# One load of v per four heads, longer runs of q, another order of keys and queries, and a planner with new figures

## The chip, the cores and the metric

The kernel runs on one core of one Trainium2 chip. The metric is device time in microseconds (us) of one execution. Engines are named as in the profile: PE is TensorE, DVE is VectorE, ACT is ScalarE, POOL is GpSimd, SP is the engine that issues most DMAs here.

## The reference

Attention over 8 batches, 12 heads, 448 positions and 64 dimensions, with q and k normalised, and then a gated two-layer network over all heads of a position, which the kernel calls MoE:

```python
q_n, k_n = rmsnorm(q, g_q), rmsnorm(k, g_k)
attn = softmax(q_n @ k_n.T / sqrt(64))          # per batch and head
x = (attn @ v) as (batch, 448, 768)
xk = mu_k * x + (1 - mu_k) * x_prev             # x_prev: one position earlier
xr = mu_r * x + (1 - mu_r) * x_prev
k = relu(xk @ w_k)                              # 768 -> 1024
out = sigmoid(xr @ w_r) * (k * k @ w_v)         # 1024 -> 768
```

The weights come as 64-bit floats and are converted on the chip.

## The kernel before

**Tiles.** A pair is two heads of one batch (48 pairs), a quad is two pairs (24 quads). The 448 positions are 7 slots of 64; position r*7 + t is row r of slot t, and a tile holds two heads in its two halves of 64 partitions. Most products are made in f16 with a high and a low part (three matmuls for one), but the first three quads (U32) run in f32. For the first six quads (PE_T) q and k are transposed by PE; after that they are split in two f16 parts and transposed by DMA.

**Stages.** These are generators, and they run side by side:

- `load` fetches a quad's k and q; `stats` squares and sums them (ACT, POOL, DVE) and makes the reciprocal root on DVE; `preps` scales them, splits them (`nat`) and transposes them into `stk`.
- `vload` fetches v of one pair into one of two tiles `vf`, with four DMAs on SP, in runs of one row (256 bytes). `vprep` squares v (ACT), brings the row sums to all partitions with a small matmul on PE, makes a power-of-two scale on DVE and splits v into `vh` and `vl`.
- `scores` makes two 128x448 score tiles per group, seven groups per quad; `expo` takes the maximum (DVE) and the exponential (ACT); `probs` and `split` normalise, split and transpose the result into `pT`, by a DMA transpose on SP or, for some groups, on PE.
- `attends` multiplies `pT` with v, one product per pair (`ot`), and ACT copies it into `x`. For the f32 pairs small matmuls (`rb`) bring the row sums and DVE multiplies by them. `mix` then forms xk and xr per pair (`df`, `xk`, `xr`).
- `wload` and `weights` fetch and convert 20 weight tiles; their DMAs are issued by ACT.
- `moe` runs the three matrix products: K (`mm<-xk,wk`), R (`mm<-wr,xr`) and V (`mm<-wv,kk`), and stores the output. K of a batch needs `xk` of its six pairs and all eight tiles of w_k; R and V of the first batch need all weights.

**What sets the order.** A planner (`Plan`) holds a clock per engine and prices every operation. Among the next operations of all generators it takes the one with the smallest start time less a priority, and appends it to its engine's program. Each engine then runs its program in that order, and waits on semaphores only. Priorities (`PRIO_`), margins (`MARGIN`) and boosts (`BOOST_`) are numbers at the head of the file, and so are leads (`LEAD_W`: the quad whose load must have begun before weights are fetched). The DMA figures, time to issue, to move and to land, stand in `emit`. Nearly all instructions are recorded by one line there (L272), so groups are told apart by their tiles. SP runs one queue: loads of q, k and v, transposes into `pT` and `stk`, and stores.

Two places of the memory matter for the change: v has `VF_BUFS` tiles `vf` and `VH_BUFS` tiles each of `vh` and `vl`; a `vf` tile is free again when its last reader is done (for f32 pairs that is the attention product itself).

Of the kernel before, what the change touches and what calls it, by code (L numbers as in the profile page):

```python
# [16 lines left out]
P = 128  # L17
HD = 64
# [6 lines left out]
NH = D_MODEL // 2  # L25
TINY = 2.0 ** -60
# [14 lines left out]
VF_BUFS = 2  # L41
# [4 lines left out]
PRIO_P = 200  # L46
PRIO_S = 150
PRIO_A = 50
PRIO_Q = 50
PRIO_V = 310  # L50
MARGIN = 600
MARGIN_A = 400
MARGIN_V = 1200
# [5 lines left out]
PRIO_O = 300  # L59
# [3 lines left out]
BOOST_R = 500  # L63
BOOST_A = 0
BOOST_W = 300
BOOST_Q = 600
SLACK_S = 3
SLACK_Q = 2
BOOST_V = 0
SLACK_V = 2  # L70
# [4 lines left out]
PRIO_L = 0  # L75
# [3 lines left out]
V_SIDE = 2  # L79
# [6 lines left out]
BOOST_F = 4000  # L86
# [4 lines left out]
LEAD_W = 1  # L91
# [3 lines left out]
W_GAP = 10e3  # L95
# [20 lines left out]
def heads(tile_, off):  # L116
    ap = tile_[:, :, :]
    return bass.AP(tensor=ap.tensor, offset=ap.offset + off, ap=[list(ap.ap[0]), [HD, 2], [2 * HD, NT], [1, HD]])
# [86 lines left out]
class Plan:  # L205
# [60 lines left out]
    def emit(self, ops):  # L266
# [18 lines left out]
        elif ops[0].fn.__name__.startswith("dma"):  # L285
# [3 lines left out]
            if "transpose" in op.fn.__name__:  # L289
                w, iss, tot = n / 128 * 1.21, 1600, 4000  # L290
            else:
                w, iss, tot = n / 55, 640, 3300
            w, tot = w * DMA_SLOW, tot * DMA_SLOW
            other = "ACT" if e == "SP" else "SP"
            if e == "ACT":
                end = s + (375 if n > 60000 else 610)
            else:
                end = max(s + iss, min(self.dma_free[e] - 1200, s + 4000))
# [122 lines left out]
def attn_moe_kernel(tc, q, k, v, g_q, g_k, mu_k, mu_r, w_k, w_v, w_r, out):  # L421
# [37 lines left out]
    NQ, NPAIR, NSS, NSL = len(quads), len(pairs), 4 * NT, (NT + 1) // 2  # L459
    VFREE = [const.tile([P, 2 * NSL, HD], F32, name="vf%d" % n) for n in range(VF_BUFS)]  # L460

# [17 lines left out]
    def late():  # L479
# [11 lines left out]
        "vh": Ring(ap_, [P, 2 * NSL, HD], F16, "vh", VH_BUFS, plan),  # L491
        "vl": Ring(ap_, [P, 2 * NSL, HD], F16, "vl", VH_BUFS, plan),
# [39 lines left out]
    def setup():  # L532
# [4 lines left out]
        for vf in VFREE:  # L537
            yield G_.memset(out=vf[HD:P, NSL - 1, :], value=0.0)
            yield G_.memset(out=vf[0:HD, NSL, :], value=0.0)
# [37 lines left out]
    def load():  # L577
        for u in range(NQ):
# [3 lines left out]
            for n, src in enumerate((k, q)):  # L582
                t = yield from R["qk"].get(u < 3)
                for x in range(2):
                    D = (A if u == 0 and (x or n == 0) else SP).dma_start
                    h0 = 4 * j + 2 * x
                    if u < PE_T or n == 0:
                        yield D(out=t[x * HD:(x + 1) * HD], in_=src[b, h0:h0 + 2].rearrange("h (r t) d -> r h (t d)", t=NT))
                    else:
                        tf = t.rearrange("p h c -> p (h c)")  # L590
                        for t0 in range(x, NT - 1, 2):
                            o = t0 // 2 * 4 * HD
                            yield D(out=tf[x * HD:(x + 1) * HD, o:o + 4 * HD].rearrange("p (h d) -> p h d", d=HD),
                                    in_=src[b, 4 * j:4 * j + 4].rearrange("h (r t) d -> r h t d", t=NT)[:, :, t0, :])
                        yield D(out=tf[x * HD:(x + 1) * HD, 12 * HD:].rearrange("p (h d) -> p h d", d=HD),
# [619 lines left out]
```

## Time and profile before

| | |
|---|---|
| median of 3 runs | 1036.73 us (1035.93 to 1038.05) |
| profiled execution, span | 1038.0 us; no time beside the span is given for it, so the span stands for its time |
| mean granted TensorE clock | 0.970 |
| busy: PE, DVE, ACT, POOL | 935.8, 788.0, 749.4, 661.0 us |
| DMA packets | 447,043, of which 418,784 are under 512 bytes |
| first MoE matmul (K) | at 166.64 us |
| start of the last attention product | at 934.35 us |

Busy time of an engine is not its limit: a matmul's end is modelled, and matmuls are pipelined. A row of waits reads: engine and tile, who released it, us in total, times, longest. A row of the timeline reads: start, duration, engine, line, operation, output and inputs, and in brackets the engine's idle time before it and who ended that. "SPq" and "ACTq" are the queues that issue DMAs.

### The profile page before, as it was taken

Reading aid. Unit: us, or ns where it says so; the run is one execution under the profiler, and the core shown is the slowest. Engines: PE = TensorE matmul, PEld = TensorE weight load, DVE = VectorE, ACT = ScalarE, POOL = GpSimd, SP = SyncE. Lnnn points to the kernel's source line nnn. Section 1 sums busy time; section 2 is a strip of 40 time slices with the busy share of each in tenths; the row PEclk is TensorE's granted clock in tenths of the full one; section 3 lists DMA queues with packets and bytes.
Section 4 is the critical chain, followed back from the end, with each engine's and each line's share of the span. In section 5 each row is a group of like instructions: output and inputs, shape, how many; then the busy total and the mean of one; then the engine's idle time right before and its main releaser. Section 6 shows DMA issues by size and latency. Waiting matters only on the chain. (4 is left out here: it accounts for less than half of the span.)

```text
span 1038.0 us, 19082 instructions
## 1 busy us (share of the span) xinstructions
PE 935.8 (90%) x6262; PEld 495.5 (48%) x6262; DVE 788.0 (76%) x1973; ACT 749.4 (72%) x1755; POOL 661.0 (64%) x696
## 2 busy tenths in 40 slices
PE   1778677879999999999999999899989999999997
PEld 1444433435554555454545544455545554555564
DVE  4898879998978897978895988779876879673000
ACT  2787657997968887888887886987887787873311
POOL 2564658936678567877677757855984757646501
PEclk9898887989999999999999999999999999999999
DMA  8543437988897999789798798799869977771011
GB/s 198 143 122 106 115 91 166 202 160 155 156 174 125 176 183 161 139 156 179 157 175 140 152 185 167 129 171 183 173 118 159 170 154 135 139 140 32 1 31 31
DMA packets 447043, 146.63 MB, mean 141 GB/s; under 512 B 418784, under 2 KB 443360, under 8 KB 446944
## 3 DMA queue, kind: packets, MB, share of 16 engines
q1 hardware_dynamic: 427408, 127.42, 65.7%
q10 hardware_dynamic: 19536, 18.00, 6.1%
q8 instruction: 49, 0.80, 0.3%
q14 instruction: 50, 0.41, 0.1%
HBM read 50.40 MB, written 11.01 MB: 59 GB/s over the span
## 5 line engine op out<-in xcount | busy, mean ns | idle before, releaser
L272 PE MATMUL mm<-wvh,kk 128*128 128x384 f16 x896 | 233.8, 326 | 0.6 <-POOL kk L272 0.4
L272 ACT ACTIVATE sc<-sc,sums 128x448 f32<-128x448 f32 x294 | 180.9, 617 | 59.2 <-DVE sums L272 54.8
L272 DVE TENSOR_REDUCE sums<-sc 128x1 f32<-128x448 f32 x336 | 194.8, 614 | 28.7 <-PE sc L272 27.9
L272 PE MATMUL mm<-xk,wkh 128*128 128x448 f16 x768 | 209.0, 354 | 3.8 <-ACT kf L272 2.6
L272 DVE SCALAR_TENSOR_TENSOR nat<-sc,sums,nat 128x448 f16<-128x448 f32 x246 | 161.2, 675 | 29.1 <-ACT nat L272 28.6
L272 ACT ACTIVATE nat<-sc,sums 128x448 f16<-128x448 f32 (+1 forms) x278 | 168.7, 648 | 14.2 <-DVE sums L272 4.9
L272 PE MATMUL mm<-wrh,xr 128*128 128x384 f16 x672 | 177.6, 329 | 0.0
L272 PEld LDWEIGHTS <-kk 128*128 128x128 f16 (+1 forms) x1362 | 129.5, 98 | 96.3 <-issue 14.4
L272 PE MATMUL sc<-stk 64*128 64x448 f16 (+3 forms) x1104 | 131.7, 385 | 22.1 <-DVE nat L272 12.7
L272 PE MATMUL mm<-wvl,kk 128*128 128x384 f16 x448 | 146.0, 326 | 0.0
L272 PE MATMUL mm<-xk,wkl 128*128 128x448 f16 x384 | 135.8, 354 | 0.0
L272 PEld LDWEIGHTS <-xr 128*128 128x128 f16 x1008 | 96.1, 98 | 73.9 <-issue 14.4
L272 PE MATMUL ot<-pT,vh 128*64 128x448 f16 x672 | 103.3, 364 | 11.1 <-DMA pT<-nat 7.4
L272 PE MATMUL mm<-wrl,xr 128*128 128x384 f16 x336 | 110.3, 328 | 0.0
L272 PEld LDWEIGHTS <-wkh 128*128 128x128 f16 x768 | 72.1, 98 | 79.1 <-issue 18.4
L272 DVE SCALAR_TENSOR_TENSOR o<-o,mm 128x384 f32<-128x384 f32 x56 | 30.7, 548 | 88.5 <-PE mm L272 58.5
L272 POOL TENSOR_TENSOR o<-o,bsc 128x384 f32<-128x384 f32 x48 | 42.9, 894 | 82.0 <-DVE o L272 49.3
L272 POOL TENSOR_TENSOR qk<-qk,ss 128x896 f32<-128x896 f32 x36 | 63.3, 1757 | 44.4 <-DVE ss L272 36.7
L272 ACT ACTIVATE o<-mm,bsc 128x128 f32<-128x128 f32 x144 | 44.6, 382 | 50.8 <-PE mm L272 38.6
L272 PEld LDWEIGHTS <-stk 64*128 64x128 f16 x1008 | 36.1, 98 | 80.2 <-issue 50.7
L272 DVE SCALAR_TENSOR_TENSOR df<-x,bsc,df 128x448 f32<-128x448 f32 x68 | 63.2, 941 | 5.4 <-POOL df L272 5.3
L272 POOL TENSOR_TENSOR nat<-nat 128x448 f32<-128x448 f32 x38 | 44.5, 1170 | 35.1 <-ACT nat L272 35.0
(169 smaller groups left out, 1784.5 us busy)
## 6 DMA issues: line engine op xcount, KB each, us to landing
out_dram<-o SPq DMA_DIRECT2D x56, 192.0 KB, 3.3
qk<-in_k_dram SPq DMA_DIRECT2D x46, 224.0 KB, 3.8
qk<-in_q_dram SPq DMA_DIRECT2D x108, 64.0 KB, 2.5
vf<-in_v_dram SPq DMA_DIRECT2D x96, 64.0 KB, 2.7
raw<-in_moe_w_v_dram ACTq DMA_DIRECT2D x12, 512.0 KB, 4.9
vf<-in_v_dram SPq DMA_DIRECT2D x96, 48.0 KB, 2.4
raw<-in_moe_w_r_dram ACTq DMA_DIRECT2D x12, 384.0 KB, 3.4
kk<-in_moe_w_k_dram ACTq DMA_DIRECT2D x8, 384.0 KB, 4.4
```

Source lines behind the costliest of these rows:

```text
L272: r = op.fn(op.kw["out"], op.kw["value"]) if op.fn.__name__ == "memset" else op.fn(**op.kw)
```

## The change

**v per quad.** One tile `vf` of a quad's size takes the place of two of a pair's size. Four DMAs load it, each for two heads in runs of 1024 or 768 bytes; one Square, one small matmul and one scale serve all four heads. `vh` and `vl` become one tile `vhl`, with two buffers still. The tile `vf` is free when both pairs are split (or, in f32, after both products and the Square).

**Order of keys and queries.** v's runs need the slots with even t side by side, then the odd ones: the order of keys (`KORD`) and of queries (`QORD`) follows. From quad 6 on q is loaded with one DMA of 768-byte runs and one of 256 per half, where there were three and one of 256. The f16 splits of k and q are made in two pieces each, and the copy of the attention product into `x` in two.

**The planner.** A transpose is priced at 1690 ns to issue and 4310 to land (1600 and 4000 before), a load at n/50 + 100 to move, 610 to issue and 2450 or 3300 to land (n/55, 640, 3300). Nearly all priorities, margins and boosts have other values, and weights are fetched one quad later (LEAD_W 2 for 1). Every engine's program comes out in another order.

```diff
-VF_BUFS = 2
+VF_BUFS = 1
-PRIO_P = 200
+PRIO_P = 447
-MARGIN_V = 1200
+MARGIN_V = 659
-LEAD_W = 1
+LEAD_W = 2
...
-                w, iss, tot = n / 128 * 1.21, 1600, 4000
+                w, iss, tot = n / 128 * 1.21, 1690, 4310
-                w, iss, tot = n / 55, 640, 3300
+                w, iss, tot = n / 50 + 100, 610, 2450 if n < 60000 else 3300
...
-                        for t0 in range(x, NT - 1, 2):
-                            o = t0 // 2 * 4 * HD
-                            yield D(out=tf[x * HD:(x + 1) * HD, o:o + 4 * HD].rearrange("p (h d) -> p h d", d=HD),
-                                    in_=src[b, 4 * j:4 * j + 4].rearrange("h (r t) d -> r h t d", t=NT)[:, :, t0, :])
+                        w = NLO * HD
+                        yield D(out=tf[xs, 0:4 * w].rearrange("p (h c) -> p h c", h=4),
+                                in_=src[b, 4 * j:4 * j + 4].rearrange("h (r t) d -> r h (t d)", t=NT)[:, :, x * w:(x + 1) * w])
...
-                yield A.copy(out=hi, in_=t4)
-                yield E_.tensor_tensor(out=lo, in0=t4, in1=hi, op=ALU.subtract)
+                for t4, hi, lo in views:
+                    yield A.copy(out=hi, in_=t4)
+                for t4, hi, lo in views:
+                    yield E_.tensor_tensor(out=lo, in0=t4, in1=hi, op=ALU.subtract)
...
-        for i in range(NPAIR):
-            b, hp = pairs[i]
+        for u in range(NQ):
+            b, j = quads[u]
             yield from until(lambda: VFREE)
             vf = VFREE.pop(0)
...
         if half:
             yield inverse(iv, sv)
-            yield A.activation(out=vh, in_=vf, func=AF.Copy, scale=sv)
-            yield V.scalar_tensor_tensor(out=vl, in0=vf, scalar=sv, in1=vh, op0=ALU.mult, op1=ALU.subtract)
+            for e in range(2):
+                if e:
+                    hl = yield from R["vhl"].get()
+                ve = vf[:, 2 * NSL * e:2 * NSL * (e + 1), :]
+                yield A.activation(out=hl[:, 0], in_=ve, func=AF.Copy, scale=sv)
+                yield V.scalar_tensor_tensor(out=hl[:, 1], in0=ve, scalar=sv, in1=hl[:, 0], op0=ALU.mult, op1=ALU.subtract)
             VFREE.append(vf)
```

Three places of the new order follow. First the head of ACT's program, before. Here `xk` and `nat` are lent as buffers: `xk_104` holds first the quad's k; `kk` and `raw` are lent for the first weight tiles.

```order
L272 DMA xk_104<-in_k_dram 64x2x448 x2
L272 ACT_TABLE_LOAD
L272 CAST ident_75<-ident 128x128
L272 DMA xk_104<-in_q_dram 64x2x448
L272 DMA kk_103<-in_moe_w_k_dram 128x3x256 x2
L272 DMA raw_135<-in_moe_w_k_dram 128x3x256
L272 DMA raw_138<-in_moe_w_k_dram 128x3x256
L272 ACTIVATE xk_104<-xk_104 128x896
L272 ACTIVATE nat_161<-xk_104 128x896
```

The same place now:

```order
L275 DMA xk_103<-in_k_dram 64x2x448
L275 ACT_TABLE_LOAD
L275 CAST ident_75<-ident 128x128
L275 DMA xk_103<-in_k_dram 64x2x448
L275 DMA xk_103<-in_q_dram 64x2x448
L275 ACTIVATE xk_103<-xk_103 128x896
L275 ACTIVATE nat_152<-xk_103 128x896
L275 DMA kk_102<-in_moe_w_k_dram 128x3x256 x2
L275 DMA raw_180<-in_moe_w_k_dram 128x3x256
```

The two Squares (of k, then of q) moved ahead of the four weight DMAs, and one half of k moved behind the cast.

Second, PE's program from the sixth attention product (`ot`) to the first K (`mm<-xk,wkh`), before. Each `sc` pair is one group of scores (6 or 12 matmuls with their weight loads, shown once), `rc` marks the `rb` matmuls, `wf` and `dg` are weight tiles.

```order
L272 MATMUL ot_1564<-pT,vf_95 64x448 x8
L272 MATMUL sc_1600<-stk_891 128x448
L272 MATMUL sc_1599<-stk_891 128x448
L272 MATMUL sc_1616<-stk_891 64x448
L272 MATMUL sc_1615<-stk_891 64x448
L272 MATMUL sc_1660<-ident,rc_107 64x128 x6
L272 MATMUL sc_1687<-stk_891 128x448
L272 MATMUL sc_1686<-stk_891 128x448
L272 MATMUL mm_1705<-wf_1552 128x128
L272 MATMUL mm_1705<-dg,ones 128x128
L272 MATMUL mm_1746<-xk_104,wkh 128x448
```

And now:

```order
L275 MATMUL ot_1512<-pT,vf_94 64x448 x8
L275 MATMUL mm_1507<-wf_1468 128x128
L275 MATMUL mm_1507<-dg,ones 128x128
L275 MATMUL sc_1527<-ident,nat_1495 128x128 x4
L275 MATMUL sc_1554<-stk_925 128x448
L275 MATMUL sc_1553<-stk_925 128x448
L275 MATMUL sc_1572<-ident,rc_106 64x2x64 x6
L275 MATMUL mm_1612<-wf_1547 128x128
L275 MATMUL sc_1620<-stk_925 64x448
L275 MATMUL sc_1619<-stk_925 64x448
L275 MATMUL mm_1612<-dg,ones 128x128
L275 MATMUL mm_1671<-xk_103,wkh 128x448
```

One group of scores stands ahead of `rb` where two stood, and two groups in all where three stood; a weight tile's matmuls and a transpose of four blocks came in ahead.

Third, SP's queue around one quad's q in the middle of the program, before:

```order
L272 DMA_TRANSPOSE stk_5207<-nat_5220 128x14x128
L272 DMA qk_5254<-in_q_dram 64x4x64 x3
L272 DMA qk_5254<-in_q_dram 64x2x64
L272 DMA_TRANSPOSE stk_5207<-nat_5296 128x14x128
L272 DMA qk_5390<-in_k_dram 64x2x448 x2
L272 DMA_TRANSPOSE pT<-nat_5209 128x14x128
```

Now:

```order
L275 DMA_TRANSPOSE stk_5156<-natx_5165 128x14x128
L275 DMA qk_5245<-in_q_dram 64x4x192
L275 DMA qk_5245<-in_q_dram 64x2x64
L275 DMA_TRANSPOSE stk_5156<-nat_5251 128x14x128
L275 DMA qk_5291<-in_k_dram 64x2x448 x2
L275 DMA_TRANSPOSE pT<-nat_5213 128x14x128
```

The rows of three q loads become one row of a single load with runs of three slots; the second half's loads repeat the first half's and are not shown.

More of the change, by code (lines that the diff above doesn't have):

```diff
@@ L25 @@
 NH = D_MODEL // 2
+NSL = (NT + 1) // 2
+NLO = NT // 2
+KORD = [t // 2 + NSL * (t % 2) for t in range(NT)]
+QORD = [t // 2 + NLO * (t % 2) for t in range(NT - 1)] + [NT - 1]
 TINY = 2.0 ** -60
@@ L671, in turn @@
                     o = column(z[:, a * P:], HD, 1)
-                ops.append(T.transpose(form=("tr", TR_COST), out=o, in_=w[:, a0 + a, :], identity=ident))
+                ops.append(T.transpose(form=("tr", TR_COST), out=o, in_=w[:, (QORD if n else KORD)[a0 + a], :], identity=ident))
             ops[0].form = ("tr", TR_COST * m)
@@ L711, in vfree @@
+            VF[u] = vf
+    def vfree(u, vf):
+        FR[u] = FR.get(u, 0) + 1
+        if FR[u] == 3:
             VFREE.append(vf)
     def vpreps():
-        i = 0
-        while i < NPAIR:
-            st["vi"] = i
-            n = V_SIDE if i < 2 * U32 else 1
-            yield from vprep([i + e for e in range(n)])
-            i += n
-    def vprep(js):
-        b, hp = pairs[js[0]]
-        n, half = len(js), js[0] >= 2 * U32
-        if hp == 0:
-            BS[b] = small.tile([P, 2 * NP], F32, name="bstat", bufs=3)
+        for u in range(NQ):
+            st["vi"] = u
+            yield from vprep(u)
@@ L726, in vprep @@
+    def vprep(u):
+        b, j = quads[u]
+        half = u >= U32
+        n = 1 if half else 2
+        NS = NP // 2 * n
+        if j == 0:
+            BS[b] = small.tile([P, 2 * NS], F32, name="bstat", bufs=3)
         s_ = BS[b]
         vs = small.tile([P, 4], F32, name="vs", bufs=4)
-        vh = vl = pt = None
-        for e, i in enumerate(js):
-            yield from until(lambda: i in VF and st["tq"] >= GATE_V)
-            vf = VF.pop(i)
-            if half:
-                vh = yield from R["vh"].get()
-                vl = yield from R["vl"].get()
-                sq = vh.bitcast(BF16)
-            else:
-                VV[i] = vf, None, None
-                pt = pt or (yield from banks["ot"].get())
-                sq = pt.rearrange("p (a c) -> p a c", c=HD)
-            yield A.activation(out=sq, in_=vf, func=AF.Square, accum_out=vs[:, e:e + 1])
-            if not half:
-                vfree(i, vf)
-                if e < n - 1:
-                    banks["ot"].put(pt)
-                    pt = None
@@ L746, in vprep @@
-        pt = pt or (yield from banks["ot"].get())
+        yield from until(lambda: u in VF and st["tq"] >= GATE_V)
+        vf = VF.pop(u)
+        hl = pt = None
+        if half:
+            hl = yield from R["vhl"].get()
+            yield A.activation(out=hl.rearrange("p a c d -> p (a c) d").bitcast(BF16), in_=vf, func=AF.Square, accum_out=vs[:, 0:1])
+            pt = yield from banks["ot"].get()
+        else:
+            for e in range(2):
+                VV[2 * u + e] = vf[:, 2 * NSL * e:2 * NSL * (e + 1), :], None, vf
+            pt = yield from banks["ot"].get()
+            for e in range(2):
+                yield A.activation(out=pt.rearrange("p (a c) -> p a c", c=HD), in_=vf[:, 2 * NSL * e:2 * NSL * (e + 1), :], func=AF.Square, accum_out=vs[:, e:e + 1])
+            vfree(u, vf)
@@ L904, in attends @@
             x = yield from R["x"].get()
[L905 removed]
+            vh, vl, own = VV.pop(i)
+            iv = None if vl is None else own[0]
             pT = PT.pop(i)
```

105 lines of the change are left out of this document (53 added, 52 removed).

## The prediction

> **What bounds the kernel now.** I read the page first, then the busy time by stage, then TensorE's waits in the early and in the long middle stage, then single stretches of the timeline.
>
> ```profile
> span 1038.0 us, 19082 instructions
> PE 935.8 (90%) x6262; PEld 495.5 (48%) x6262; DVE 788.0 (76%) x1973; ACT 749.4 (72%) x1755; POOL 661.0 (64%) x696
> ```
>
> TensorE (PE) is busy for 90% of the span, so 102 us is all that any order of the work can win without removing matmuls. The table of stages says where these 102 us lie:
>
> ```profile
> core 0: us, PE busy (x) PEld busy (x) DVE busy (x) ACT busy (x) POOL busy (x), PEclk, DMA share, GB/s
> 0.00:21.30 21.30, 0.00 (x0) 0.03 (x1) 9.68 (x39) 5.61 (x10) 5.62 (x16) 1.00 0.80 197
> 21.30:166.60 145.30, 107.73 (x674) 61.22 (x675) 124.61 (x359) 99.98 (x231) 83.99 (x94) 0.86 0.47 124
> 166.60:210.00 43.40, 36.89 (x249) 18.35 (x249) 40.20 (x85) 38.58 (x81) 38.18 (x40) 0.96 0.83 183
> 210.00:234.00 24.00, 17.36 (x122) 8.91 (x122) 23.01 (x70) 21.44 (x49) 7.85 (x10) 0.87 0.79 155
> 234.00:480.00 246.00, 239.94 (x1646) 124.65 (x1642) 208.16 (x503) 198.30 (x472) 174.12 (x174) 0.99 0.87 158
> 480.00:720.00 240.00, 228.58 (x1579) 118.33 (x1578) 197.88 (x487) 193.67 (x456) 166.67 (x169) 0.99 0.89 164
> 720.00:936.70 216.70, 209.61 (x1440) 108.96 (x1435) 170.69 (x417) 169.03 (x405) 147.57 (x155) 0.99 0.79 148
> ```
>
> Span less PE busy gives the idle time of each: 21.3 us before the first transpose, 37.6 us up to the first MoE matmul at 166.6, 13.1 us in the next two stretches together, and 6.1 + 11.4 + 7.1 = 24.6 us in the 702.7 us from 234 to 936.7. The rest, 5.7 us, lies at the very end. Up to 166.6 it is VectorE (DVE) that sets the pace: it is busy 124.61 of 145.3 us (86%) while PE has 74%. From 234 on PE is 96.5% busy and sets the pace itself. Its waits, first from 21 to 167 us, then from 234 to 937:
>
> ```profile
> PE sc L272 <- DVE nat L272: 29.9, 6, 21.3
> PE ot L272 <- DVE dg L272: 4.5, 1, 4.5
> PE sc L272 <- POOL nat L272: 4.2, 3, 1.8
> ```
> ```profile
> PE ot L272 <- DMA pT<-nat: 6.6, 8, 1.4
> PE sc L272 <- DVE nat L272: 5.3, 9, 1.2
> PE sc L272 <- DMA stk<-nat: 4.0, 4, 2.6
> ```
>
> The 29.9 hold the 21.3 us of the start. In the middle stage 10.6 of the 24.6 us are waits for DMA transposes.
>
> The other end of the program is fixed: from the last attention product on, PE runs matmuls alone.
>
> ```profile
> 936.74 88.78 PE mm L272 x522
> ```
>
> Both orders keep nearly the same work behind the last attention product: 564 matmuls then and 570 now, of which this row of the chain holds 522. So the total is PE's work plus PE's idle time, and each edit is priced by what it does to these two.
>
> **Part by part. The start.** The first transpose waits for q's sums of squares:
>
> ```profile
> 0.73 1.40 ACTq L272 DMA_DIRECT2D xk<-in_k_dram  x2
> 9.04 2.01 ACTq L272 DMA_DIRECT2D raw<-in_moe_w_k_dram  x2
> 11.10 0.95 ACT L272 ACTIVATE xk<-xk 128x896 f32<-128x896 f32 x1 [7.34 <-DMA kk<-in_moe_w_k_dram]
> xk<-in_k_dram ACTq DMA_DIRECT2D x2, 224.0 KB, 6.2
> 13.29 0.62 DVE L272 TENSOR_REDUCE sst<-xk 128x14 f32<-128x448 f32 x1 [2.59 <-POOL xk L272]
> 16.42 0.61 DVE L272 TENSOR_REDUCE sst<-nat 128x14 f32<-128x448 f32 x1
> 21.30 1.73 PE L272 MATMUL sc<-ident,nat 128*128 128x128 f32 x7 [21.30 <-DVE nat L272]
> ```
>
> The k tile was asked for at 0.73 and its second half 0.7 later; with 6.2 us to landing it is there by 7.6. Yet the first Square starts at 11.10, right behind the weight DMAs that ACT issues until 11.05. In the new order those four issues stand behind both Squares. One of the two k issues now stands behind the identity's cast; even if that costs it 1 us, k lands by 8.6 and its Square starts 2.5 us sooner. On DVE the small instructions on the gains no longer stand split around k's reduction, so q's reduction moves from 16.42 by about as much. I take **2.5 us** off the start; the ends are 0 (q's own half, issued last, lands as late as before) and 4.
>
> **Up to the first MoE matmul.** Counted in the two orders, the last mixing instruction of batch 0 on DVE (the sixth that writes `df`) is its instruction 388 before and 366 now: scores, a normalisation and a half-precision v of later quads moved behind it. By the stage's row an instruction of DVE takes 124.61/359 = 0.347 us, so 22 fewer are 7.6 us of DVE, 8.9 us of a stage in which DVE is 86% busy. Two more rows show how PE ends this stage:
>
> ```profile
> 159.47 1.96 PE L272 MATMUL sc<-ident,rc 128*64 128x128 f32 x16 [5.05 <-DVE nat L272]
> 166.64 0.90 PE L272 MATMUL mm<-xk,wkh 128*128 128x448 f16 x2 [0.38 <-DVE WSC L272]
> ```
>
> The `rb` matmuls of the sixth pair, which release its mixing, waited 5.05 us for a PSUM bank that DVE's splits held, because 18 score matmuls (two groups, four banks) stood in front. In the new order one group of 6 stands in front. On the other side, nine more weight matmuls and two more half weight tiles come ahead of the first MoE matmul, and what is postponed must be done later, where DVE is busy 40.20 of 43.40 us. There the MoE's R and V matmuls become available earlier in the program (after 96 attention matmuls in place of 144), so PE has something to fill with. I take **6 us**, between nothing and 10.
>
> **DMA and SP's queue, 234 to 937 us.** A quad's q took eight issues and takes four; its v took eight and takes four.
>
> ```profile
> q1 hardware_dynamic: 382610, 109.37, 84.7%
> qk<-in_q_dram SPq DMA_DIRECT2D x102, 64.0 KB, 2.5
> vf<-in_v_dram SPq DMA_DIRECT2D x72, 64.0 KB, 2.7
> pT<-nat SPq DMA_TRANSPOSE x108, 4.6
> ```
> ```profile
> L272 SPq DMA_DIRECT2D vf<-in_v_dram x192: 595/614/1560, 2.4 to 900.5; - x192
> L272 SPq DMA_TRANSPOSE pT<-nat x123: 1322/1866/3709, 153.8 to 928.8; - x123
> ```
>
> The transposes stand in the same queue as these loads. Eight issues less of 0.614 us per quad, over about 17 quads of this stage, take some 84 of 703 us from SP. The 16 DMA engines are busy 84.7% of the time with 382,610 packets, 24.9 ns of one engine each. Packets of v fall from 1792 to 512 per quad, of q from 1792 to 768: 39,000 fewer in 17 quads. If a packet costs the same whatever its size, that is 61 us of all 16 engines (9% of the stage); if only bytes count, nothing. Of PE's 10.6 us of waits for transposes I take **4 us** off, between 0 and 10.6; nearer the low end, because a transpose takes 1.87 us to issue and 4.6 us to land whatever stood before it.
>
> The Trainium skill, page "DMA: Bandwidth & Descriptors", section "Why small descriptors are slow (HBM only)", charges every packet about 3 cycles on top of one per 32 bytes, 11 for 256 bytes. By that a run of 768 bytes takes 27 cycles in place of 33, and these loads would keep 82% of their DMA time: an estimate from that page of 17 us of all engines in place of 61, and by it I would take 1 us here in place of 4, which makes the sum 12.5 and the time 1024. No row of this trace separates the two.
>
> **v's statistics.** One chain per quad replaces two, 21 times. PE loses 21 small matmuls:
>
> ```profile
> 181.87 0.22 PE L272 MATMUL ot<-ident,vs 128*128 128x128 bf16 x1
> 182.02 0.74 PE L272 MATMUL sc<-stk 64*128 64x448 f16 x6
> L272 DVE TENSOR_REDUCE vs<-ot 128x1 f32<-128x128 f32 x42 | 11.8, 280 | 6.2 <-PE ot L272 6.2
> ```
>
> The next matmul starts 0.15 us after it, and it can take its whole 0.22: 3.2 to 4.6 us of PE's own time. I take **3 us**. DVE loses 21 reductions of 0.280 and three small instructions with each, some 12 us spread over 700; DVE is 82% busy there, so I count nothing (at most 3 us less).
>
> **What is added.** Splitting the f16 copies of k and q (two pieces each, 18 quads) gives ACT and GpSimd (POOL) 36 instructions more each; the copy out of the attention product gives ACT 24 more; the one Square per quad takes 21 away.
>
> ```profile
> L272 ACT CAST nat<-qk 128x896 f16<-128x896 f32 x28 | 27.0, 965 | 3.8 <-POOL qk L272 2.1 <-POOL x L272 1.6
> L272 ACT CAST xk<-df 128x448 f16<-128x448 f32 x34 | 19.5, 578 | 5.8 <-DVE df L272 5.6
> L272 POOL TENSOR_TENSOR nat<-qk,nat 128x896 f16<-128x896 f32 x28 | 53.6, 1914 | 18.4 <-ACT nat L272 16.4 <-DVE nat L272 1.6
> L272 POOL TENSOR_TENSOR xk<-df,xk 128x448 f16<-128x448 f32 x34 | 37.9, 1116 | 17.3 <-ACT xk L272 13.7 <-DVE natx L272 3.5
> ```
>
> Two halves cost 2 x 578 - 965 = 191 ns more on ACT and 2 x 1116 - 1914 = 318 ns more on POOL: 39 x 0.191 = 7 us of ACT and 36 x 0.318 = 11 us of POOL in some 800 us. ACT is busy 80% and POOL 70% of the middle stage, and the pieces stand a quad ahead of the scores that need them: nothing, and up to 4 us if that lead is gone.
>
> **The sum.** 2.5 + 6 + 4 + 3 = 15.5 us off 1038.0, that is 1022.5 for the profiled execution, whose span stands 1.3 us over the runs' median of 1036.73. So **1021 us** for the median. Less than 0.2% (2 us) is what a measurement of this kernel cannot tell from no change.
>
> **The rivals.** *One v buffer on a shared queue.* Two v tiles of a pair become one of a quad. Its load may start only when the second pair's last read is done, and it waits at the head of SP's queue with transposes behind it. Four issues and a landing are 4 x 0.614 + 2.7 = 5.2 us. The 42 half-precision attention products between 166.6 and 936.7 come 18.3 us apart on average, which covers this, and in the order the two products of a quad stand close with a long gap to the next quad. But if the planner releases loads too early on SP, 5.2 us shows at each late quad: from three quads of 21 on the sum is eaten, with five it is 26 us, so 1021 + 26 = 1047. The Trainium skill, page "Trainium Kernel Development and Optimization", section "Best Practices", speaks for this rival: double-buffer, so that DMA and compute overlap; no row of this trace shows a load without its second buffer. I give it 0.13.
>
> *The gain is taken back.* The start (2.5) and the matmuls (3) hold, the rest is eaten by the postponed DVE work: 1031. For it speaks DVE's 93% right after 166.6. 0.17.
>
> *No net gain,* new waits in the new order cancelling it: 1037. 0.08.
>
> *More than forecast:* all terms at their upper ends, 4 + 10 + 10.6 + 4.6 = 29, or most of it: 1007 to 1012. 0.10.
>
> **How the numbers follow.** The forecast, 1021 with 1013 to 1029 of its own, has 0.52. Below 1010 and above 1040 I leave about 0.06 and 0.11; so 1010 to 1040. Faster is the forecast, the half gain and the large gain, 0.52 + 0.17 + 0.10 = 0.79; same 0.08; slower 0.13.
>
> **What would show it.** Right: the first transpose near 19 us and the first MoE matmul at 155 to 160; PE idle between 234 and the last attention product under 21 us, its waits for `pT` and `stk` transposes under 7; q1's share in that stage below 80%. Wrong: the first MoE matmul at 165 or later (the second term), waits of PE or ACT for `vf` DMAs or for `vh`/`vhl` that grow (the first rival), or PE idle over 25 us in the middle stage.

## The result and the profile after

The changed kernel takes **1002.68 us** (median of 4 runs, 998.37 to 1003.91) where the kernel before took 1037.39 beside it (4 runs, 1035.93 to 1040.87): a ratio of 0.9649, 95% interval 0.9622 to 0.9677. The forecast was 1021 with a range from 1010 to 1040, so the sign was right and the size, 15.5 us, less than half of the 35. The profiled execution took 998.37 us, 2 more than its span. It is the shortest of the four: the two profiled spans lie 41.6 us apart where the medians lie 34.7. The page begins:

```profile
span 996.4 us, 18699 instructions
PE 926.0 (93%) x6241; PEld 487.4 (49%) x6241; DVE 777.6 (78%) x1890; ACT 749.7 (75%) x1772; POOL 675.9 (68%) x732
```

The busy time by stage, cut at the first transpose, the first MoE matmul and the last matmul of the last attention product, and between them near the cuts of before, 200 for 210 among them (stretch, its length, then busy time per engine, granted clock, DMA share, GB/s):

```profile
0.00:18.91 18.91, 0.00 (x0) 0.03 (x1) 10.82 (x39) 5.78 (x9) 5.11 (x14) 1.00 0.77 198
18.91:151.00 132.09, 104.68 (x670) 59.74 (x671) 118.39 (x330) 94.08 (x216) 84.01 (x95) 0.90 0.51 138
151.00:200.00 49.00, 40.88 (x263) 20.59 (x262) 45.38 (x108) 42.49 (x88) 36.62 (x38) 0.96 0.73 163
200.00:234.00 34.00, 33.38 (x253) 18.33 (x251) 30.36 (x83) 30.90 (x78) 19.19 (x21) 1.00 0.81 150
234.00:480.00 246.00, 245.12 (x1699) 125.72 (x1698) 213.16 (x505) 208.99 (x504) 183.71 (x196) 1.00 0.92 172
480.00:720.00 240.00, 235.46 (x1611) 119.81 (x1610) 204.81 (x476) 203.81 (x487) 189.14 (x199) 1.00 0.91 169
720.00:893.80 173.80, 169.62 (x1187) 87.45 (x1181) 140.48 (x333) 140.82 (x341) 119.86 (x130) 1.00 0.80 151
893.80:996.40 102.60, 96.91 (x574) 55.69 (x570) 14.21 (x21) 22.82 (x55) 38.23 (x42) 0.99 0.10 24
```

The span fell by 41.6 us: 2.4 in the start, 13.2 up to the first MoE matmul (145.3 to 132.1), 27.0 up to the last attention product (769.8 to 742.8, with its last matmul at 936.4 and at 893.8), and 1.0 came back at the end. From 234 us on PE is idle for 9.6 us where it was for 24.6. Over the whole span its idle time went from 102.2 to 70.3 us, and its busy time from 935.8 to 926.1.

TensorE's waits, first from 18.91 to 151 us, then from 151 to 893 us (us in total, times, longest):

```profile
PE sc L275 <- DVE nat L275: 19.2, 2, 18.9
PE mm L275 <- DVE wf L275: 7.3, 3, 3.3
PE mm L275 <- DVE dg L275: 3.6, 4, 2.0
```
```profile
PE mm L275 <- ACT kf L275: 6.4, 2, 3.9
PE sc L275 <- DVE nat L275: 4.5, 8, 1.2
PE sc L275 <- POOL nat L275: 1.5, 3, 1.0
PE ot L275 <- ACT vhl L275: 1.2, 2, 0.7
PE ot L275 <- DMA pT<-nat: 1.2, 2, 0.6
```

The 19.2 hold the 18.9 us of the start. The waits for DMA transposes, 10.6 us from 234 us on before, are down to 1.2. The queue of the loads, in the stretch from 234 us to the last product:

```profile
q1 hardware_dynamic: 336215, 108.25, 87.8%
```

Packets are fewer (382,610 before), but the share of the DMA engines rose from 84.7% to 87.8%: 27.6 ns for a packet in place of 24.9. Times the length of the stretch, the queue's packets took 579 us of all 16 engines where they took 595; the stretch itself shrank by 43.

### The profile page after: what moved, and what is told of

It is laid out like the page before. It is cut to its first block, busy times and chain, and to the rows that moved or that the text cites. A ratio compares the mean times of both kernels' runs of the same rounds, so it can differ in the third digit from the quotient of the medians.

```text
span 996.4 us, 18699 instructions
## 1 busy us (share of the span) xinstructions
PE 926.0 (93%) x6241; PEld 487.4 (49%) x6241; DVE 777.6 (78%) x1890; ACT 749.7 (75%) x1772; POOL 675.9 (68%) x732
## 3 DMA queue, kind: packets, MB, share of 16 engines
q1 hardware_dynamic: 375568, 127.41, 67.4%
## 5 line engine op out<-in xcount | busy, mean ns | idle before, releaser
L275 ACT ACTIVATE sc<-sc,sums 128x448 f32<-128x448 f32 x294 | 182.1, 623 | 47.0 <-DVE sums L275 43.1
L275 ACT ACTIVATE nat<-sc,sums 128x448 f16<-128x448 f32 (+1 forms) x276 | 163.0, 647 | 22.3 <-DVE sums L275 16.1
L275 DVE SCALAR_TENSOR_TENSOR nat<-sc,sums,nat 128x448 f16<-128x448 f32 x242 | 154.6, 676 | 22.8 <-ACT nat L275 22.0
L275 PE MATMUL ot<-pT,vhl 128*64 128x448 f16 x1008 | 103.7, 354 | 2.9 <-DMA pT<-nat 1.2
L275 DVE SCALAR_TENSOR_TENSOR o<-o,mm 128x384 f32<-128x384 f32 x56 | 30.7, 548 | 89.1 <-PE mm L275 55.2
L275 POOL TENSOR_TENSOR qk<-qk,ss 128x896 f32<-128x896 f32 x36 | 62.8, 1745 | 32.4 <-DVE ss L275 26.5
L275 PEld LDWEIGHTS <-vhl 128*64 128x64 f16 x1008 | 54.7, 110 | 48.5 <-issue 8.9
L275 DVE SCALAR_TENSOR_TENSOR df<-x,bsc,df 128x448 f32<-128x448 f32 x68 | 71.2, 1057 | 8.3 <-POOL df L275 8.2
L275 POOL TENSOR_TENSOR nat<-qk,nat 128x768 f16<-128x768 f32 (+3 forms) x58 | 62.7, 1094 | 11.5 <-ACT nat L275 11.2
```

What stands on the lines that cost most here:

```text
L275: r = op.fn(op.kw["out"], op.kw["value"]) if op.fn.__name__ == "memset" else op.fn(**op.kw)
```

## The experiments

Two accounts stood against each other at the start. *Loads:* the new layout gives the gain through SP's queue or the packets, and the prediction priced it too low. *Order:* the planner's new numbers give it, and the layout little. A third held that v's statistics are worth more than 3 us. Measured, each beside the kernel before on the same chip; PE's idle time is a stretch's length less PE busy, in the four stretches (start, to the first MoE matmul, to the last attention product, behind it), and the last column counts PE's matmuls from the last one of the last product on. The last four columns are of the one profiled execution, which need not be the median one (that of e7 is its longest):

| run | median us (range, runs) | ratio, 95% interval | first MoE at | PE busy | PE idle | behind |
|---|---|---|---|---|---|---|
| before | 1037.39 (1035.93–1040.87, 4) | | 166.6 | 935.8 | 21.3+37.6+37.7+5.7 = 102.2 | 568 |
| after | 1002.68 (998.37–1003.91, 4) | 0.9649, 0.9622–0.9677 | 151.0 | 926.1 | 18.9+27.4+18.3+5.7 = 70.3 | 574 |
| e1_layout_only | 1033.71 (1030.33–1037.6, 10) | 0.9969, 0.9953–0.9985 | 171.9 | 936.9 | 20.9+38.6+32.0+5.7 = 97.2 | 570 |
| e2_planner_only | 1070.56 (1069.17–1076.33, 4) | 1.0338, 1.0304–1.0372 | 163.7 | 949.3 | 13.2+44.8+55.2+6.0 = 119.1 | 580 |
| e5_old_dma_figures | 1048.02 (1044.22–1049.58, 4) | 1.0106, 1.0072–1.0140 | 170.1 | 940.9 | 18.8+39.5+40.8+5.8 = 104.9 | 796 |
| e6_old_priorities | 1035.65 (1033.03–1039.73, 10) | 0.9996, 0.9978–1.0015 | 170.8 | 935.7 | 20.4+39.0+31.5+5.9 = 96.9 | 574 |
| e3_old_runs_same_order | 1066.22 (1061.18–1074.51, 4) | 1.0293, 1.0237–1.0349 | 153.4 | 947.6 | 18.7+27.8+67.7+5.7 = 119.8 | 574 |
| e7_q_old_runs | 1036.69 (1033.42–1044.4, 10) | 1.0014, 0.9988–1.0040 | 156.9 | 941.8 | 18.9+28.7+47.5+5.7 = 100.8 | 574 |
| f1_q_three_long | 1040.97 (1037.94–1048.44, 10) | 1.0021, 0.9999–1.0044 | 153.8 | 935.8 | 18.8+27.9+48.1+5.7 = 100.4 | 574 |
| e8_v_two_issues | 1019.83 (1017.94–1022.47, 4) | 0.9841, 0.9809–0.9874 | 151.1 | 934.0 | 18.3+28.7+33.9+5.7 = 86.7 | 576 |
| e14_v_half_on_act | 1002.32 (999.29–1008.55, 4) | 0.9666, 0.9627–0.9704 | 151.7 | 930.8 | 18.1+26.7+20.0+5.7 = 70.5 | 574 |
| f6_q_tail_on_act | 1000.93 (999.98–1002.4, 4) | 0.9650, 0.9621–0.9678 | 152.1 | 928.2 | 19.1+28.5+18.6+5.7 = 71.8 | 574 |
| e4_v_chain_twice | 1006.58 (1004.54–1010.0, 4) | 0.9721, 0.9694–0.9748 | 151.8 | 930.1 | 19.3+27.9+19.8+5.6 = 72.6 | 576 |
| e10_margin_580 | 1005.07 (1002.5–1010.09, 4) | 0.9700, 0.9667–0.9733 | 150.1 | 926.6 | 19.0+28.6+20.7+5.7 = 74.1 | 616 |
| f3_w_gap_5000 | 1013.52 (1011.45–1015.48, 4) | 0.9760, 0.9737–0.9784 | 148.8 | 929.6 | 19.1+29.0+26.3+5.7 = 80.0 | 622 |
| f5_w_gap_6800 | 1016.47 (1014.82–1018.6, 4) | 0.9793, 0.9760–0.9827 | 159.4 | 933.7 | 18.9+32.2+25.9+6.1 = 83.1 | 706 |
| f2_w_gap_old | 1032.92 (1031.43–1035.17, 5) | 0.9943, 0.9924–0.9962 | 149.1 | 934.0 | 18.9+31.5+43.1+5.8 = 99.2 | 706 |
| f4_lead_l_old | 1035.51 (1029.78–1039.38, 10) | 0.9964, 0.9946–0.9982 | 172.3 | 936.9 | 21.0+40.5+27.3+5.7 = 94.5 | 706 |
| e12_start_numbers_old | 1031.53 (1030.48–1033.67, 4) | 0.9942, 0.9921–0.9963 | 147.3 | 933.8 | 20.8+28.2+41.3+6.1 = 96.4 | 742 |
| e13_middle_numbers_old | 1031.07 (1027.48–1033.17, 4) | 0.9931, 0.9904–0.9958 | 178.1 | 943.5 | 19.0+36.0+25.7+5.7 = 86.5 | 498 |

### The two halves of the change

**e1_layout_only**: the new layout of v, q, keys and queries, with the planner of before.

```diff
 # all in the changed kernel; VF_BUFS stays 1
-LEAD_W = 2
+LEAD_W = 1
-W_GAP = 6679.939
+W_GAP = 10e3
...
-                w, iss, tot = n / 50 + 100, 610, 2450 if n < 60000 else 3300
+                w, iss, tot = n / 55, 640, 3300
```

> The changed kernel (v per quad, long runs of q, two-piece splits, new order of keys and queries) under the planner's old figures: all priorities, margins, boosts, leads and DMA figures as before. Theory A (the planner's figures make the gain, by an order with fewer waits of PE): most of the gain is gone, 1025 to 1040 us. Theory B (fewer and longer DMAs make it, by freeing SP's queue and the DMA engines) and theory C (the shorter v chain on DVE and PE makes it): most of the gain stays, 1000 to 1012.

**e2_planner_only**: the kernel before with the planner's new numbers (`VF_BUFS` stays 2).

```diff
 # all in the kernel before
-LEAD_W = 1
+LEAD_W = 2
...
-                w, iss, tot = n / 55, 640, 3300
+                w, iss, tot = n / 50 + 100, 610, 2450 if n < 60000 else 3300
```

> The kernel of before with the planner's new figures, all that fit it (two v tiles of a pair stay). Theory A: most of the gain, 1003 to 1015 us. Theories B and C: little of it, 1028 to 1040.

The layout alone gives 4 us, the planner alone loses 33, both together win 35. Neither account holds as it stood: the parts do not add. The new numbers fit the new layout, though; whether others would bring the old layout as far was not tried.

**e5_old_dma_figures** and **e6_old_priorities** split the planner's half, with the new layout in both: e5 puts back the DMA figures in `emit` alone, e6 the sixteen numbers at the head alone (five of the twelve priorities, three margins, four boosts, two slacks, `LEAD_W` and `W_GAP`).

```diff
 # e5
-                w, iss, tot = n / 128 * 1.21, 1690, 4310
+                w, iss, tot = n / 128 * 1.21, 1600, 4000
...
-                end = max(s + iss, min(self.dma_free[e] - 805, s + 4000))
+                end = max(s + iss, min(self.dma_free[e] - 1200, s + 4000))
```
```diff
 # e6
-MARGIN = 560
+MARGIN = 600
...
-W_GAP = 6679.939
+W_GAP = 10e3
```

> The changed kernel with one thing undone: the DMA figures in the planner (1600 and 4000 for a transpose, n/55, 640 and 3300 for a load, 1200 of lead) as before; all priorities new. Theory F (the new figures make the order good, because it counts SP's time and the landings as they are): most of the 31 us between the layout alone (1033.7) and the changed kernel (1002.7) are lost, 1020 us or more. Theory G (the priorities make it): 1000 to 1012.

> The changed kernel with the new DMA figures and all priorities, margins, boosts and leads as before. Theory F: 1000 to 1015 us. Theory G: 1022 or more.

With either half put back nearly the whole gain is gone or more, 45 us in e5 and 33 in e6, and the first MoE matmul is back at 170 us. So the figures and the numbers belong to each other as layout and planner do.

### What the loads are worth in the new order

Here the order of instructions on PE, DVE, ACT and POOL is that of the changed kernel, and only DMA issues are split at their place in SP's program. The edit in `emit` is one for all four runs:

```diff
-            with self.tc.issue_after(self.last[e].ins) if e in self.last else nullcontext():
-                r = op.fn(op.kw["out"], op.kw["value"]) if op.fn.__name__ == "memset" else op.fn(**op.kw)
-            self.last[e] = r
+            for kw in getattr(op, "pieces", [op.kw]):
+                with self.tc.issue_after(self.last[e].ins) if e in self.last else nullcontext():
+                    r = op.fn(kw["out"], kw["value"]) if op.fn.__name__ == "memset" else op.fn(**kw)
+                self.last[e] = r
```

**e7_q_old_runs** splits each long load of q into three of 256-byte runs, **e8_v_two_issues** each load of v into one per head (its runs stay long), and **e3_old_runs_same_order** does both:

```diff
 # e7, in load
+op.pieces = [{k: y[:, :, a * HD:(a + 1) * HD] for k, y in op.kw.items()} for a in range(NLO)]
 # e8, in vload
+op.pieces = [{k: y.rearrange("p x (c d) -> p x c d", d=HD)[:, a, :, :] for k, y in op.kw.items()} for a in range(2)]
```

> The changed kernel with every engine's order untouched, but each of its q loads from quad 6 on issued as three with runs of one slot, and each v load as two (one per head), so that SP issues as many DMAs as before the change (168 more, some 100 us of SP's time at 0.61 us each). Theory B: half of the gain or more is lost, 1018 us or more, with PE waiting for transposes into pT and stk as before (11 us in the long stage). Theories A and C: within 5 us of the changed kernel, 1000 to 1008.

> The changed kernel with every engine's order untouched; only q's loads from quad 6 on are issued as three with runs of one slot (72 issues more, 18,432 packets more); v as changed. Both old shapes together cost 63 us. Theory D (what costs is SP's time to issue, which delays the transposes behind): 72 of 168 extra issues, so some 27 us, 1025 to 1035. Theory E (what costs is the short packets on the DMA engines, which only q had back): nearly all of the 63 us, 1055 or more.

> The changed kernel with every engine's order untouched; only v's loads are issued as two each, one per head (96 issues more, the same packets); q as changed. Theory D: 96 of 168 extra issues, so some 36 us, 1030 to 1045. Theory E: within 6 us of the changed kernel, 1000 to 1009.

The 168 issues of e3 cost 63 us; the 72 of q alone 34, the 96 of v alone 17, which lies between the two expectations. In e7, though, packets grew with the issues. **f1_q_three_long** adds the same 72 issues with the runs left at 768 bytes, split by heads:

```diff
+op.pieces = [{k: y[:, a:z, :] for k, y in op.kw.items()} for a, z in ((0, 2), (2, 3), (3, 4))]
```

> Same order on every engine; each load of q in runs of 768 bytes is issued in three parts (heads 0 and 1, head 2, head 3), so SP has 72 more issues and q1 not one packet more. The run with four issues and 256-byte runs had the same 72 more issues and 18,432 more packets, and took 1036.69 us, 34 more than the changed kernel. Theory D (issues): 1028 to 1040, as there. Theory E (packets: the short runs are what costs): 1003 to 1010. Theory M (both; an issue costs what it cost on v, 0.18 us): 1003 + 13 = 1013 to 1020.

It costs 38 us, no less than e7. The row of the loads' queue over the whole program, of e7 and then of f1, says that the short runs' 18,432 packets are not there (the changed kernel has 375,568, and 72 more DMAs bring 1,152 of their own):

```profile
q1 hardware_dynamic: 395152, 127.42, 64.6%
```
```profile
q1 hardware_dynamic: 376720, 127.42, 64.8%
```

So it is the added issues in SP's queue, not the short runs. Where they strike is seen at one quad. SP's timeline of the changed kernel, then of f1:

```profile
378.78 2.04 SPq L275 DMA_TRANSPOSE stk<-nat  x1
380.87 3.08 SPq L275 DMA_DIRECT2D qk<-in_q_dram  x4
384.61 1.53 SPq L275 DMA_TRANSPOSE stk<-nat  x1
```
```profile
393.93 2.08 SPq L276 DMA_TRANSPOSE stk<-nat  x1
396.06 5.68 SPq L276 DMA_DIRECT2D qk<-in_q_dram  x8
401.84 1.56 SPq L276 DMA_TRANSPOSE stk<-nat  x1
```

q's loads stand between the two transposes of a quad. Four issues hold the second transpose back for 3.1 us, eight for 5.7, and the transpose then goes out 7.9 us after the first in place of 5.8. PE's timeline of f1 there (start, duration, and in brackets the idle time before and who ended it):

```profile
402.52 0.54 PE L276 MATMUL mm<-xk,wkh 128*128 128x448 f16 x2
...
403.19 2.46 PE L276 MATMUL ot<-pT,vhl 128*64 128x448 f16 x24
407.75 0.77 PE L276 MATMUL sc<-stk 64*128 64x448 f16 x6 [2.10 <-DMA stk<-nat]
408.46 0.93 PE L276 MATMUL mm<-xk,wkh 128*128 128x448 f16 x2
...
410.67 0.95 PE L276 MATMUL mm<-xk,wkh 128*128 128x448 f16 x2
...
411.77 0.54 PE L276 MATMUL mm<-xk,wkh 128*128 128x448 f16 x2
```

PE has waited 2.10 us for the second `stk`. Then the next matmul pairs take 0.93 to 0.95 us in place of 0.54, for 3.3 us. The stretches around it show the granted clock (the last but two of the columns):

```profile
395.00:403.00 8.00, 8.00 (x48) 3.95 (x45) 7.43 (x13) 7.91 (x18) 7.87 (x9) 1.00 0.72 133
403.00:407.70 4.70, 2.65 (x26) 1.27 (x24) 4.70 (x9) 3.60 (x8) 4.70 (x5) 1.00 1.03 212
407.70:411.70 4.00, 3.95 (x15) 1.55 (x16) 2.93 (x6) 1.07 (x3) 2.22 (x3) 0.58 1.29 216
411.70:420.00 8.30, 8.30 (x58) 3.85 (x58) 5.83 (x14) 7.83 (x18) 7.71 (x9) 1.00 0.92 180
```

The clock is 0.58 on average after the wait (0.50 from 408.33 to 411.75) and 1.00 again from there on. In 3.3 us at 0.95 a pair PE does what takes 1.9 at 0.54, so the wait of 2.1 us costs another 1.4. The groups by form show the sum of it, the score products of the changed kernel and of f1 (count, busy, mean ns, idle before):

```profile
L275 PE MATMUL sc<-stk 64*128 64x448 f16 x756 | 91.5, 353 | 5.7 <-DVE nat L275 4.7 <-ACT pT L275 0.6 <-DVE bsc L275 0.2
```
```profile
L276 PE MATMUL sc<-stk 64*128 64x448 f16 x756 | 93.2, 358 | 26.4 <-DMA stk<-nat 12.0 <-DVE nat L276 10.5 <-DMA stk<-natx 2.5
```

Of the 20.7 us that are added here 14.5 wait for `stk` by name; another 5.8 are put down to DVE's `nat`. Over the whole program PE's idle time grew by 30.1 us.

Is there more to be had by the same way? **e14_v_half_on_act** lets ACT issue 48 of v's 96 loads (for the second head of each pair), **f6_q_tail_on_act** the 36 short loads of q, in the same order:

```diff
 # e14, in vload, for the second head of a pair; f6 the same in load, for slot 6
+op.via, op.on = nc.scalar.dma_start, "ACT"
 # both, in emit: via in place of op.fn, and on in place of e as the key of last
```

> Same order of instructions on PE, DVE, ACT and POOL; 48 of the 96 loads of v (every second pair) are issued by ACT in place of SP, at the same place in the order. SP is relieved of 48 issues of 0.65 us = 31 us. Theory D (the time that issues take in SP's queue is what the new order lives on; 96 more v issues cost 17 us, 0.18 each): SP's relief gives 48 x 0.18 = 9 us back if the relation goes on below the present number, less what 48 issues cost ACT, 48 x 0.4 to 0.6 us = 19 to 29 us of an engine that is 75% busy: 993 to 1000. Theory F (at the present number SP's queue has ended to be a limit; the relation is one-sided): no gain, and ACT's issues delay its exponentials: 1003 to 1015. Theory Q (ACT waits at its place in order for v's buffer to come free, and everything behind it waits too): over 1020, with PE waiting on ACT for over 30 us in the long stage.

> Same order on every engine; the 36 short loads of q (the seventh row of each token, 32 KB) are issued by ACT in place of SP. Theory D downwards (72 more issues cost 38 us, 0.53 each, and the relation goes on below the present number): 36 x 0.53 = 19 us less, of which ACT's 36 issues of some 0.5 us take up to 18 back: 985 to 998. Theory F (one-sided: SP's queue has enough slack as the order stands, the order was planned with these issues in it): 1000 to 1008. Theory Q (ACT waits for q's tile to come free and its exponentials stand behind it): over 1012, PE waiting on ACT.

Both are as fast as the changed kernel, and neither is faster. ACT takes 0.60 us for each issue instead, yet PE's waits for ACT's `vhl` hardly move (1.2 us in the changed kernel, 1.6 and 1.2 here); PE's waits for transposes were only 1.2 us to begin with. SP's queue is one-sided: issues beyond those that the order was written for cost 0.18 (v) to 0.53 us (q) each, and moving some away gives nothing.

**e4_v_chain_twice** tries the third account: v's statistics are issued twice (matmul, reduction, first scale and inverse), so that as much stands there as before, with the same order.

```diff
 # in vprep, for f16 quads
+op.pieces = [op.kw, op.kw]
```

> The changed kernel with every engine's order untouched, but the small steps of each half-precision v (matmul for the row sums, reduction, first scale step, inverse) issued twice, so that PE and DVE have as many of them as before the change (21 matmuls, 63 DVE instructions, 12 us of DVE). Theory C: at least 10 us longer, 1013 or more. Theories A and B: longer by PE's own 3 to 5 us at most, 1003 to 1008.

It costs 3.9 us, far from the 35. The account falls.

### Which numbers of the planner

**e12_start_numbers_old** and **e13_middle_numbers_old** put back four and twelve of the sixteen numbers:

```diff
 # e12; e13 is the other twelve
-LEAD_W = 2
+LEAD_W = 1
-PRIO_L = 192
+PRIO_L = 0
-W_GAP = 6679.939
+W_GAP = 10e3
-BOOST_W = 248
+BOOST_W = 300
```

> The changed kernel with four of the planner's numbers put back, those that time the first weights (LEAD_W 1, PRIO_L 0, W_GAP 10e3, BOOST_W 300). With all sixteen put back the kernel took 1035.65 us, 33 us more than the changed one, and its first MoE matmul began at 170.8 us in place of 151.0. Theory S (the numbers work by place): these four make the early start of the MoE and nothing else, so the first MoE matmul is back at 168 to 172, PE's idle time in the long stage stays at 18 to 22 us, and the time is 1003 + 17 = 1017 to 1023. Theory J (one joint fit: any part put back spoils the order everywhere): PE's idle time in the long stage rises to 28 us or more too, and the time is 1028 to 1045. Theory N (these four do nothing by themselves): 1000 to 1008, first MoE matmul by 155.

> The complement: the other twelve numbers put back (margins, priorities, slacks, boosts of the long stage), the four for the first weights kept. Theory S: the first MoE matmul stays at 150 to 155, PE's idle time in the long stage rises from 18.3 to the 31.5 us that it had with all numbers put back, time 1003 + 13 to 18 = 1015 to 1022. Theory J: the early start is lost too (first MoE matmul after 160) and the time is 1028 to 1045. Theory N': the twelve are what matters, and all of the 33 us come back with the first MoE matmul still early: 1030 to 1040.

Each loses 28 to 29 us, and all sixteen together lose 33. No account by place holds: in e12 the first MoE matmul is earlier than ever, at 147.3, and the loss is behind it (41.3 us of idle time for 18.3). In e13, whose numbers were to act in the long stage, the first MoE matmul is at 178.1.

**f2_w_gap_old** and **f4_lead_l_old** split the four again, and **f3_w_gap_5000**, **e10_margin_580** and **f5_w_gap_6800** move one number by a step:

```diff
-W_GAP = 6679.939
+W_GAP = 10e3        # f2; f3: 5000; f5: 6800
-MARGIN = 560
+MARGIN = 580        # e10
-LEAD_W = 2
+LEAD_W = 1          # f4, with PRIO_L = 0
```

> The changed kernel with the weights' pace alone put back (W_GAP 6680 to 10000, so the planner presses weight tiles less the longer it runs). Theory P (the pace is what fills TensorE behind the first MoE matmul): the first MoE matmul stays within 5 us of 151, PE's idle time between there and 250 us rises from 9 to 20 us or more, more than 640 matmuls are left behind the last attention product (570 in the changed kernel), and the time is 1018 to 1032. Theory L (the other two numbers of the start carry it): 1000 to 1010.

> The two numbers of the start alone put back (LEAD_W 2 to 1, PRIO_L 192 to 0): the first weights are asked for ahead of the second quad's q and k again. Theory L: the first transpose is back at 20.5 to 21.5 us, and the long stage loses as it did with all four put back: 1020 to 1032. Theory P: the start loses its 2 us and little else: 1003 to 1010.

> The pace moved on by half of the change's step, 6680 to 5000. Theory P with room left: PE's idle time in the second stage falls below 27 us and the time is 990 to 1000. Theory O (the change's value is near its best; weights that come earlier push attention's DVE work back): 1003 to 1020, PE waiting more for nat and sums.

> The changed kernel with one number, MARGIN, moved from 560 to 580 (before: 600). The order is the same until the middle of the program; from there instructions stand in other places on all engines. Theory J (the order is a narrow optimum: any neighbouring order is worse by some part of the 33 us): 1008 to 1025, with PE's idle time in the long stage at 24 us or more. Theory W (the numbers sit on a broad slope, so that a third of the step from 600 to 560 costs next to nothing): 1000 to 1006. Both keep the first MoE matmul at 150 to 153.

> The changed kernel with the weights' pace moved by 2%, 6680 to 6800; nothing else. The planner then writes another order on all engines from the second stage on. Theory G (the number works by its size): of the 30 us that the step to 10000 cost, 2% to 4% come back, about 1 us: 1002 to 1006. Theory R (the order is one of many that differ by the whole spread of the other runs; the numbers pick one): anywhere from 1008 to 1036, most likely 1012 to 1032, with PE's idle time behind the first MoE matmul over 25 us.

The pace alone loses 30 us, the other two alone 33, more than either expectation for them, and both with `BOOST_W` 29. A step of the pace either way loses: 11 us at 5000 and, with a step of 2%, 14 us at 6800. e10, whose order parts from the changed kernel's only in the middle of the program, is unresolved against it (1002.5 to 1010.09). How f2 and f5 lose is seen behind the first MoE matmul, up to 250 us, in the changed kernel, f2 and f5:

```profile
151.00:250.00 99.00, 90.11 (x616) 47.06 (x615) 89.95 (x224) 87.15 (x197) 64.67 (x69) 0.98 0.81 165
```
```profile
149.10:250.00 100.90, 73.26 (x457) 35.25 (x459) 86.21 (x208) 78.44 (x166) 64.44 (x67) 0.81 0.80 164
```
```profile
159.40:250.00 90.60, 79.12 (x501) 39.13 (x502) 78.48 (x190) 72.80 (x162) 53.22 (x58) 0.91 0.66 142
```

PE is idle for 8.9, 27.6 and 11.5 us, and its clock is 0.98, 0.81 and 0.91. The work that did not run there stands at the end. f5 starts its last attention product at 892.3 us, earlier than the changed kernel, but has more behind it:

```profile
892.30:1016.80 124.50, 118.37 (x706) 68.59 (x702) 18.84 (x27) 27.21 (x68) 45.55 (x52) 1.00 0.09 23
```

706 instructions of PE and 124.5 us, for 574 and 102.6. MoE matmuls that could have filled PE's waits earlier run alone at the end.

## Why the prediction was wrong

**The start** was right, and in its mechanism: 2.5 us forecast, 2.4 measured. The first Square starts at 8.96 us where it started at 11.10, and q's reduction at 13.36 where it stood at 16.42. In f4, whose numbers put four weight issues ahead of the Squares again, the first Square is at 12.01 and the first transpose at 21.04. **What is added** was rightly put at nothing: PE waits for `vhl` on ACT for 1.2 us (for `vh`, 0.5 before) and for POOL's `nat` for 1.5, as before.

**v's statistics** came near in number, 3 forecast and 3.9 in e4, but that they are PE's own time for 21 matmuls is not borne out: the clock, below, accounts for what PE's busy time gained in e4.

**"Up to the first MoE matmul"** failed in its size: 6 us with an end at 10, against 13.2. DVE's work in the stage fell by 6.2 us (124.61 to 118.39), near the 7.6 that the moved instructions were priced at. But DVE's idle time in the stage fell by 7.0 as well (20.7 to 13.7). The step let idle time fall only in proportion, by 1.3 (7.6 to 8.9), and then took 6 of the 8.9; the new order removed both. The wait that it read in the `rb` matmuls, 5.05 us on DVE's `nat` before, is gone as it said. The row of the changed kernel shows none:

```profile
142.41 1.14 PE L275 MATMUL sc<-ident,rc 128*64 128x128 f32 x16
```

**"DMA and SP's queue"** failed most: 4 us with an end at 10.6, in a stage that gave 27.0. With the 3 of v's statistics the forecast had 7 there. The upper end was taken from PE's waits that name a transpose, as if these were all that the queue can cost, and the low value from a transpose that takes its time whatever stood before it. In f1 four more issues ahead of a quad's second transpose move it back by 2.1 us (7.9 behind the first in place of 5.8). The named waits did go (10.6 to 1.2), so this part alone, 9.4 us, came close to the upper end. Beyond it, waits that name DVE's `nat` fell as well. From the first MoE matmul to the last attention product they were, before:

```profile
PE sc L272 <- DVE nat L272: 10.6, 13, 4.4
```

They are 4.5 now, and in f1's row above they grow again with SP's issues. Yet the waits for transposes alone do not make the time: in e6 they are down to 3.2 us in this stage, and it takes 1035.65. In the change itself PE's idle time in this stage fell from 37.7 to 18.3 us, and which part the layout has in that and which the order, no run separates. The packets, on which the step spent half of its arithmetic, are not the price: f1 and e7 differ by 18,432 packets and take 1040.97 and 1036.69 us. The Trainium skill, page "DMA: Bandwidth & Descriptors", section "Why small descriptors are slow (HBM only)", charges each packet a fixed part, from which the prediction estimated 17 us less time of all 16 engines. The rows agree: 16 us less, 595 to 579. But the forecast of 1024 that was drawn from it is as wrong as 1021, since that time did not decide.

**The sum** failed as a method. It took each edit's price by itself, in the order as it was. e1 and e2 show -4 and +33 for the halves of a change that brings -35, and e12 and e13 show +29 and +28 for two parts of what is worth 33 together. The sixteen numbers and the DMA figures select one order; of the selections tried near it e10 is no slower that these runs can tell, and all others lose 11 to 45 us. A range for such a change has to hold that spread; mine held only the ends of four terms.

**A missing term** is the clock. The sum let PE's own work change by v's 3 us alone, and PE's busy time fell by 9.7. In the runs with the changed kernel's order PE does the same matmuls, and its busy time grows with its idle time: 926.1 at 70.3, 934.0 at 86.7 (e8), 935.8 at 100.4 (f1), 941.8 at 100.8 (e7), 947.6 at 119.8 (e3); e14, with 930.8 at 70.5, shows a scatter of some 5 us. Each us of idle time brings 0.3 to 0.5 us of slower matmuls. The sums of all stretches up to the last stage with a granted clock of 0.50, seven before and five after, say the same:

```profile
sum 61.44, PE 44.55 PEld 22.86 DVE 50.26 ACT 38.50 POOL 32.27; mean PE 6.36 PEld 3.27 DVE 7.18 ACT 5.50 POOL 4.61
sum 30.73, PE 24.11 PEld 14.44 DVE 26.93 ACT 16.87 POOL 20.61; mean PE 4.82 PEld 2.89 DVE 5.39 ACT 3.37 POOL 4.12
```

PE was busy for 44.6 us at half the clock before and for 24.1 after. If a matmul takes twice its time there, half of that is the slower clock, and PE's work at full clock is an estimated 913.5 us before and 914.0 after, and by the same sum 914.1 to 916.9 in the other runs with this order. So the 9.7 us are the clock, to within some 3 us. In e4, with the 21 matmuls more, PE is busy for 32.4 us at half the clock, which leaves 913.9: what these matmuls take by themselves is lost in the scatter.

**The rivals.** One v buffer on a shared queue (1047, 0.13) did not come: in the whole program only ACT waits for v's loads, 2.1 and 0.2 us (4.7 and 2.0 us on ACT before, with two buffers), in these rows of the changed kernel's waits:

```profile
ACT ot L275 <- DMA vf<-in_v_dram: 2.1, 1, 2.1
ACT vhl L275 <- DMA vf<-in_v_dram: 0.2, 1, 0.2
```

So the Trainium skill's advice to double-buffer, on the page "Trainium Kernel Development and Optimization", section "Best Practices", did not decide here. The gap between a quad's splits and the next need covered the load. The rival that lay nearest, more than forecast, ended at 1007 since it added the same ends. Of the signs, the first transpose (18.9), PE's idle time from 234 on (9.6, under 21) and the waits for transposes (1.2, under 7) came as told; the first MoE matmul at 151 was better than 155 to 160, and q1's share below 80% was wrong (87.8%).

**What stays open.** Why this order and not its neighbours: the runs show where they lose (PE's idle time behind the first MoE matmul, and matmuls left for the end), not which property of an order would foretell it. Two v tiles of a quad's size were not tried, nor other numbers for the old layout, so that the gain needs the new layout is not shown.

## What to carry over

Where a scheduler's numbers choose the order, price the whole order and not the edits: put back halves of such a change before believing a cause, and give the forecast the spread of neighbouring orders, here some 30 us of 1000. In a queue that carries both loads and what PE waits for next, count the issues that stand between two dependent transfers; 72 more of them cost 38 us here where the bytes stood still and the packets nearly so. And price waits of TensorE at more than their length.

## What the runs showed of the hardware

- **After a wait of 2.1 us the matmuls were slow.** In f1 the clock was 0.50 for 3.42 us and a pair of matmuls took 0.95 us for 0.54. Not every wait does this: PE waited for `stk` eleven times in f1, for up to 2.1 us, and from 190 us to 1030 the clock fell twice. The Trainium skill, page "TensorE: Matmul & The Clock Gate", section "What's actually happening", tells of half rate after an idle window of about 3.4 us and of full rate after as much sustained work. The 3.3 us of slow matmuls agree; the idle time ahead of them is shorter here: of the 3.41 us before, PE was busy for 1.31.
- **The granted clock knows two values here.** In every kept trace it is 1.00 or 0.50, and its stretches at 0.50 between the first and the last stage last 3.41 us or a multiple of it: before, 3.41 twice, 6.83 twice, 10.24, 13.65 and 17.07.
- **Packets got dearer as they got fewer:** 24.9 ns before, 27.6 after, at 84.7% and 87.8% of the DMA engines. At least in part the longer runs take longer each: e7 and f1 move the same bytes in the same order, f1 with 18,432 packets fewer, and the queue's packets take 673.5 and 671.5 us of all 16 engines (27.3 and 28.5 ns each).
- **An issue on SP has no fixed price.** By the time that it takes it is 0.60 to 0.65 us (medians of loads of v in e8 and after); in the total it was worth 0.53 us between two transposes that PE waits for (f1), 0.18 us as a load of v (e8), and nothing when moved to ACT (e14, f6).
